# Other places in SBUF for the first row tiles of a kernel's last stage, and its last DRAM sums issued later

## The chip, the cores and the metric

The kernel runs on one core of a Trainium2 chip. The metric is the device time of one execution in microseconds. The core's engines work in parallel, each through its own instruction queue in order: TensorE (PE, matmuls, with its weight loads shown as PEld), VectorE (DVE), ScalarE (ACT), GpSimd (POOL) and SyncE (SP). In this kernel SP issues nearly all loads (DMA queue q1), and POOL issues stores and DRAM-to-DRAM transfers (DMA queue q0); 16 DMA engines carry them out.

## The reference, cut to what matters

```python
def _A_ref(x, dft_seq_re, dft_seq_im, dft_hid_re, dft_hid_im):
    a = jnp.einsum("bsd,ed->bse", x, dft_hid_re)
    b = jnp.einsum("bsd,ed->bse", x, dft_hid_im)
    return jnp.einsum("ts,bse->bte", dft_seq_re, a) - jnp.einsum("ts,bse->bte", dft_seq_im, b)

def _B_ref(x, W_gate, W_up, W_down):
    gate = jnp.einsum("bsd,df->bsf", x, W_gate)
    up = jnp.einsum("bsd,df->bsf", x, W_up)
    gate = gate * (gate > 0)
    h = gate * up
    return jnp.einsum("bsf,fd->bsd", h, W_down)

xn = _layernorm(x, axis=-1)
return x + _A_ref(xn, ...) + _B_ref(xn, ...)
```

Here x is 1 x 2048 x 640 (S=2048 tokens, D=640), and the gate has F=1728 columns. All is float32.

## The kernel before, in words

Every float32 product is made of three matmuls on split operands (`mm3`, lines 139 to 141): an operand is written as a high part (an ACT copy to fp32r, line 133) and a low part (a DVE subtraction, line 134), and high x high, high x low and low x high are added up in PSUM. One such split is a pair of instructions, first on ACT, then on DVE. On top of that the products are formed by a Strassen-like scheme with seven block products in place of eight (named B11, T1, T2, B21, B22, T3, T4), whose operands are sums and differences of blocks.

The work has three stages. **The first** computes the products with the sequence DFT, in four column chunks of 512 tokens; its results go to DRAM as `pq`. **The second**, the gate, runs 26 units (`gate_up(n)`, n = 0 to 25): 13 column blocks of F for the token half q=1, then 13 for q=0. Each unit loads weights into `z` (two pools, `z0` and `z1`, by turns), splits them into `gw0` or `gw1`, runs its products against the token sets, and POOL stores the result `ob` to `hd`. A remainder of F is done by `gate_up_rest`, at the beginning for q=1 and at the end for q=0. During the gate the weights of the last stage are prepared in tiles of pool `prep` and stored to `wparts` and `wquads` in DRAM. Near its end `lead_load` and `lead_split` (DVE, line 134, `gw<-st`) prepare unit 0 of the last stage from two tiles of pool `stage`.

**The last stage** (`project(q)`, first q=1, then q=0) multiplies `pq` and `hd` by the hidden DFT and by W_down. The contraction goes over seven units u: three of `hid`, two of `f`, one odd, and again `f` (in the code `UNITS`: hid (0,1), hid (2,3), hid (4), f (0,1), odd, f (2,3), f (4,5)). For each product name these seven units run in turn: for q=1 B11, T1, T2, B22 and so on. In TensorE's order unit 0 of B11 is the one from `lead_split`. A unit loads its row tile (`rw`, for the odd unit `ro`; lines 1249 to 1255) and its weights (`wt`, line 1281), DVE forms the difference of two rows (line 1304), and rows and weights are split into `cb` (a ring of four tiles, `ring2`) and `wt`. Finished sums are added to `y` on DVE (line 1217), and `y` is stored. Besides, `second_level` adds seven further products that read DRAM tiles `grown`, sums of `hd` blocks which POOL makes with accumulating DRAM-to-DRAM transfers (`grow`, lines 1144 and 1145).

The order in the last stage is written by hand for SP, POOL and PE (`drive_last`, a manual schedule): step by step, each unit's loads are issued six units ahead of its products and its splits are placed three units ahead. ACT and DVE are left to a scheduler, which decides at build time where the splits stand between the gate's last instructions. What an SP load waits for is set by two things: which of eight completion counters it takes over, and whose tile lay at its place in SBUF before.

SBUF is filled by pools that lie behind one another, left and right; a pool that opens later may lie over closed ones, and a tile then waits for the last reader of what it covers. By the sizes in the code (bytes per partition, from the end of pool `keep`) the left side during the gate is: gw0 0 to 17,408, stage to 25,600, r1 to 58,368, prep to 82,944, z0 to 92,672, wr to 97,792, tmp to 108,032, hob to 116,224, stage3 to 124,416, sets to 157,184, z1 to 166,912. When all of these are closed, the last stage puts over them: lead (six row tiles of 4,096, for B11's rows) 0 to 24,576, a gap, wts (seven weight tiles of 6,144) from 25,600 to 68,608, ring2 (four tiles of 8,192) to 101,376, raws (21 tiles of 4,096) to 187,392. Unit 0's row takes the highest place of `lead`, over both tiles of `stage`, and unit 1's the lowest, over gw0. The `odd` pool lies on the right, over the token set B22 in `xs_early`, which `gate_up_rest(0)` reads to its end.

Of the kernel before, what the change touches and what calls it, by code (L numbers as in the profile page):

```python
# [7 lines left out]
F32 = mybir.dt.float32  # L8
# [4 lines left out]
P = 128  # L13
S, D, F = 2048, 640, 1728
KD = D // P
CH = 512
# [16 lines left out]
AHEAD = 6  # L33
# [3 lines left out]
B11, B12, B21, B22, T1, T2, T3, T4, X4 = range(9)  # L37
# [28 lines left out]
def fnet_reglu_kernel(  # L66
# [15 lines left out]
    nc = tc.nc  # L82
# [18 lines left out]
    sets = [dram_p.tile([NSET, P, W2], F32, name=f"set{q}") for q in range(2)]  # L101
# [7 lines left out]
    grown = [dram_p.tile([4, P, n, CH], F32, name=f"grown{g}") for g, (_, _, n, _) in enumerate(GROUPS)]  # L109
# [44 lines left out]
    todo = []  # L154
# [681 lines left out]


    ph2 = ExitStack()
    for n, b, side in (("prep", 2, "left"), ("z0", 1, "left"), ("wr", 1, "left"), ("tmp", 1, "left"), ("hob", 2, "left"),
                       ("stage3", 2, "left"), ("sets", 1, "left"), ("z1", 1, "left"), ("gw1", 1, "right")):  # L840
        open_pools[n] = ph2.enter_context(tc.tile_pool(name=n, bufs=b, side=side, reuse_waits="tile"))
    pool = open_pools.__getitem__
    stage3 = lambda: pool("stage3").tile([P, W2], F32, name="st")
# [36 lines left out]
    tmp = lambda name, n=CH: pool("tmp").tile([P, n], F32, name=name)  # L880
# [12 lines left out]
    ending = []  # L893
# [203 lines left out]
    lead = {}  # L1097
# [36 lines left out]
    def quarter(q, g, half):  # L1134
        what, k, n, _ = GROUPS[g]
        if what == "hid":
            return pqd[2 * q][1][:, k + half * n : k + half * n + n]
        first = 2 * (k + half * n) + 1
        return hd[q][first : first + 2 * n - 1 : 2, :, :CH].rearrange("f p t -> p f t")

    def grow(g):

        t = [grown[g][i] for i in range(4)]
        put = lambda o, i: lambda: nc.gpsimd.dma_start(o, i)
        add = lambda o, i: lambda: nc.gpsimd.dma_start(o, i, accum_op=OP.add)
        return {"1": put(t[0], quarter(1, g, 0)), "1+": add(t[0], quarter(0, g, 0)), "3": put(t[2], quarter(0, g, 1)),
                "3+": add(t[2], quarter(0, g, 0)), "2": put(t[1], t[0]), "2+": add(t[1], quarter(0, g, 1)),
                "4": put(t[3], t[1]), "4+": add(t[3], quarter(1, g, 1))}

    behind_store = {n: [] for n in range(NU)}  # L1150
    for g, plan in enumerate((((10, "1 3"), (11, "1+"), (12, "3+"), (13, "2"), (14, "2+"), (15, "4"), (16, "4+")),
                              ((17, "1"), (18, "1+"), (19, "2"), (21, "3"), (22, "2+"), (23, "3+"), (24, "4"), (25, "4+")),
                              ((20, "1"), (24, "1+"), (25, "2"), (None, "3 2+ 3+ 4 4+")))):
        made = grow(g)
        for n, names in plan:
            (ending if n is None else behind_store[n]).extend(made[i] for i in names.split())
# [24 lines left out]
    ph0.close()  # L1181


    for n, b, side in (("lead", 6, "left"), ("gap", 1, "left"), ("wts", AHEAD + 1, "left"), ("ring2", 4, "left"), ("raws", 21, "left"),
                       ("odd", 4, "right"), ("y", 1, "right")):
        open_pools[n] = ctx.enter_context(tc.tile_pool(name=n, bufs=b, side=side, reuse_waits="tile"))

# [20 lines left out]
    def get_y(q, *which):  # L1208
        for e, c in which:
            own = f"{q}" if e in (0, 1, 4) and c == 0 else ""  # L1210
            y[q, e, c] = t = pool("y").tile([P, CH], F32, name=f"y{e}{c}{own}")
            nc.sync.dma_start(t, xt[e * P : (e + 1) * P, (2 * q + c) * CH : (2 * q + c + 1) * CH])
# [18 lines left out]
    def project(q):  # L1231
        c0, c1 = 2 * q, 2 * q + 1
        raws = {}
# [5 lines left out]
        def get(kind, u):  # L1239
            what, ks = UNITS[u]  # L1240
            if what == "odd":
                o = raws[kind, u] = pool("odd").tile([P, 1, CH], F32, name="ro")
            else:
                o = raws[kind, u] = pool("lead" if kind == "B11" else "raws").tile([P, 2, CH], F32, name="rw")[:, : len(ks)]
            col, row = int(kind in ("B12", "B22")), int(kind in ("B21", "B22"))
            if what == "odd":
                cs = slice(col * CH, (col + 1) * CH)
                if row:
                    nc.sync.dma_start(o[:REST, 0], hrest[q][:, cs])
                else:  # L1250
                    nc.sync.dma_start(o[:, 0], hd[q][NF - 1][:, cs])
            elif what == "hid":
                nc.sync.dma_start(o, pqd[(c0, c1)[col]][row][:, ks[0] : ks[-1] + 1])
            else:
                nc.sync.dma_start(o, hd[q][2 * ks[0] + row : 2 * ks[-1] + row + 1 : 2, :, col * CH : (col + 1) * CH].rearrange("f p t -> p f t"))

        def unit(name, u, first, last):
# [7 lines left out]
            def load():  # L1265
                kind = {"B11": "B11", "T1": "B12", "T3": "B21"}.get(name)
                if kind and (kind, u) not in raws and (name, q, u) != ("B11", 1, 0):
                    get(kind, u)
                ahead = {("T1", 2): 0, ("T1", 4): 1, ("T1", 6): 2, ("T2", 0): 3, ("T2", 2): 4, ("T2", 3): 5, ("T2", 4): 6}.get((name, u))
                if ahead is not None:  # L1270
                    get("B22", ahead)
                if (q, name, u) == (1, "B11", 1):
                    get("B11", 0)
                if q and name == "T2" and u in (1, 5):
                    get("B21", SINGLE[u // 5])
# [136 lines left out]
        for name, us in (("B11", every), ("T1", every), ("T2", every), ("B22", every[:4]), ("T3", every), ("B22", every[4:]), ("T4", every)):  # L1412
            for u in us:
# [5 lines left out]
                for kind, i, first, last in now:  # L1419
                    l, p, r, f = unit(kind, i, first, last)  # L1420
# [89 lines left out]
    alone = lambda f: (f, idle, idle, idle, idle)  # L1510
    quads = second_level()
    Y_AFTER = {(1, "T2", 5): ((4, 0),), (1, "T4", 5): ((0, 0), (1, 0))}
    for q in (1, 0):
        for steps, of in project(q):
            todo.extend(steps)
            if of in Y_AFTER:
                todo.append(alone((lambda which: lambda: get_y(0, *which))(Y_AFTER[of])))
            if of[:2] == (1, "T2") and ending:
                todo.append(alone(ending.pop(0)))
            if of in QUADS_AFTER:  # L1520
                todo.append(quads.pop(0))
    assert not quads and not ending
    with tc.manual_schedule(engines={mybir.EngineType.SP, mybir.EngineType.Pool, mybir.EngineType.PE}):
        drive_last()

# [38 lines left out]
```

## Time and profile before

| | |
|---|---|
| median of 3 runs | 1030.7 us (1030.24 to 1031.24) |
| profiled execution | 1031.5 us |
| its span (first to last instruction) | 1029.7 us |
| PE busy | 1020.5 us, 99% of the span |
| DVE busy | 824.8 us, 80% |
| ACT busy | 456.2 us, 44% |
| POOL busy | 117.8 us, 11% |
| mean granted TensorE clock | 0.996 |
| HBM read and written | 203.26 and 72.89 MB, 268 GB/s over the span |

The span is what the trace covers; the execution's own time is a little longer. "Busy" counts an engine's arithmetic, not the time in which it issues DMAs or waits on semaphores. A row of the timeline gives start, duration, engine, line and operation with output and input tiles, the number of instructions, and in brackets the idle time before it with what ended it. Matmuls are pipelined: one is shown 0.39 us long, and the next starts before it ends, so the rate is read from start to start. A row of waits gives engine, line and tile, what it waited for, the total in us, how often, and the longest. Issue rows of SP and POOL (SPq, POOLq) stand at the time of the issue, and a stretch merged into one row (x2) contains the waiting between its issues.

### The profile page before, as it was taken

How to read it: one execution, taken by the hardware profiler on the slowest of the kernel's cores; microseconds unless marked ns; L12 is line 12 of the kernel's file. 1: busy time of each engine (PE TensorE's matmuls, PEld its weight loads, DVE VectorE, ACT ScalarE, POOL GpSimd, SP SyncE). 2: the span in 40 equal slices, each digit the busy share in tenths (PEclk: the TensorE clock that was granted, in tenths of full speed). 3: DMA queues.
4: the chain of work that ended last, by engine and by line, in shares of the span. 5: the costliest groups of instructions: out<-in, count | busy, mean ns of one | idle time of the engine just before them, and what ended most of it. 6: DMA issues, size and time to landing. Idle time of an engine off the chain costs nothing.

```text
span 1029.7 us, 12759 instructions
## 1 busy us (share of the span) xinstructions
PE 1020.5 (99%) x4510; PEld 842.6 (82%) x4510; DVE 824.8 (80%) x1162; ACT 456.2 (44%) x588; POOL 117.8 (11%) x190
## 2 busy tenths in 40 slices
PE   9999999999999999999999999999999999999998
PEld 7888888888888888888888888888787888888887
DVE  7957977979879697778988878876388878598887
ACT  6664453333334443434446444443343555454552
POOL 2000010122110001321111111111100000000001
PEclk9999999999999999999999999999999999999999
DMA  9884744967859566775568889897797689999795
GB/s 333 326 271 161 261 158 126 358 224 233 333 200 364 198 206 201 246 247 187 221 223 282 283 304 337 288 316 206 223 395 260 208 265 311 325 323 324 219 282 167
DMA packets 113808, 267.57 MB, mean 260 GB/s; under 512 B 13104, under 2 KB 58096, under 8 KB 112112
## 3 DMA queue, kind: packets, MB, share of 16 engines
q1 hardware_dynamic: 92272, 178.77, 51.8%
q0 software_dynamic: 21040, 87.57, 24.6%
q8 instruction: 35, 0.57, 0.2%
q10 hardware_dynamic: 432, 0.43, 0.1%
q14 instruction: 29, 0.24, 0.1%
HBM read 203.26 MB, written 72.89 MB: 268 GB/s over the span
## 4 chain that ended last, share of the span: by engine, by line
PE 94%; DMA 3%; DVE 2%; ACT 1%; issue 0%; SPq 0%; ACTq 0%
PE ps L140 30%; PE ps L141 30%; PE ps L139 30%; PE ps L527 3%; DMA wt<-wparts 2%; PE ps L556 1%; DMA rw<-pq 1%; PE ps L1360 1%; DVE rw L1304 0%; DMA raw<-in_dft 0%; DVE cb L134 0%; DVE wt L134 0%; DVE y L1217 0%; DVE gw L134 0%; ACT cb L133 0%
## 5 line engine op out<-in xcount | busy, mean ns | idle before, releaser
L140 PE MATMUL ps<-cb,wt 128*128 128x512 f32 (+1 forms) x407 | 159.6, 392 | 2.2 <-DVE cb L134 2.1
L139 PE MATMUL ps<-cb,wt 128*128 128x512 f32 (+1 forms) x407 | 159.4, 392 | 1.8 <-ACT cb L133 1.8
L141 PE MATMUL ps<-cb,wt 128*128 128x512 f32 (+1 forms) x407 | 159.1, 391 | 0.0
L133 ACT ACTIVATE cb<-rw 128x1024 fp32r<-128x1024 f32 (+1 forms) x94 | 89.6, 961 | 87.0 <-PE ps L141 50.7
L134 DVE TENSOR_TENSOR cb<-rw,cb 128x1024 fp32r<-128x1024 f32 (+1 forms) x94 | 102.7, 1102 | 23.8 <-ACT cb L133 23.1
L133 ACT ACTIVATE cb<-raw 128x1024 fp32r<-128x1024 f32 x64 | 67.9, 1060 | 104.4 <-PE ps L141 98.0
L134 DVE TENSOR_TENSOR cb<-raw,cb 128x1024 fp32r<-128x1024 f32 x64 | 78.2, 1222 | 30.1 <-ACT cb L133 29.8
L139 PE MATMUL ps<-xs_early,gw 128*128 128x512 f32 x260 | 101.2, 389 | 0.0
L141 PE MATMUL ps<-xs_early,gw 128*128 128x512 f32 x260 | 101.2, 389 | 0.0
L140 PE MATMUL ps<-xs_early,gw 128*128 128x512 f32 x260 | 101.1, 389 | 0.0
L140 PEld LDWEIGHTS ps<-cb,wt 128*128 128x128 f32 x407 | 77.1, 189 | 19.9 <-DVE cb L134 4.1
L139 PEld LDWEIGHTS ps<-cb,wt 128*128 128x128 f32 x407 | 77.1, 189 | 18.7 <-ACT cb L133 2.6
L139 PE MATMUL ps<-cb,xs_late 128*128 128x512 f32 x232 | 90.2, 389 | 0.0
L140 PE MATMUL ps<-cb,xs_late 128*128 128x512 f32 x232 | 90.2, 389 | 0.0
L141 PE MATMUL ps<-cb,xs_late 128*128 128x512 f32 x232 | 90.2, 389 | 0.0
L141 PEld LDWEIGHTS ps<-cb,wt 128*128 128x128 f32 x407 | 77.1, 190 | 15.7
L139 PE MATMUL ps<-cb,xs_early 128*128 128x512 f32 x226 | 87.9, 389 | 0.0
L140 PE MATMUL ps<-cb,xs_early 128*128 128x512 f32 x226 | 87.9, 389 | 0.0
L141 PE MATMUL ps<-cb,xs_early 128*128 128x512 f32 x226 | 87.9, 389 | 0.0
L130 ACT ACTIVATE gw<-z 128x1024 fp32r<-128x1024 f32 (+1 forms) x52 | 56.4, 1110 | 37.1 <-PE ps L141 23.6
L130 ACT ACTIVATE u<-ps 128x512 f32<-128x512 f32 x52 | 31.1, 598 | 88.1 <-PE ps L141 74.2
L875 DVE TENSOR_TENSOR gw<-z,gw 128x1024 fp32r<-128x1024 f32 (+1 forms) x52 | 64.8, 1284 | 1.9 <-ACT gw L130 1.8
(209 smaller groups left out, 1990.7 us busy)
## 6 DMA issues: line engine op xcount, KB each, us to landing
raw<-in_dft SPq DMA_DIRECT2D x94, 512.0 KB, 5.8
wt<-wparts SPq DMA_DIRECT2D x74, 256.0 KB, 4.5
wparts<-pw POOLq DMA_DIRECT2D x12, 1408.0 KB, 7.2
z<-in_wgu SPq DMA_DIRECT2D x26, 640.0 KB, 6.1
rw<-hd SPq DMA_DIRECT2D x27, 512.0 KB, 6.6
hd<-ob POOLq DMA_DIRECT2D x26, 512.0 KB, 4.5
wt<-wparts SPq DMA_DIRECT2D x29, 384.0 KB, 5.3
rw<-pq SPq DMA_DIRECT2D x19, 512.0 KB, 5.9
```

Source lines behind the costliest of these rows:

```text
L130: return nc.scalar.activation(o, i, AF.Copy)
L133: nc.scalar.activation(hi, src, AF.Copy)
L134: return nc.vector.tensor_tensor(lo, src, hi.bitcast(F32), op=OP.subtract)
L139: nc.tensor.matmul(ps, wh, mh, start=first, stop=False, skip_group_check=more)
L140: nc.tensor.matmul(ps, wh, ml, start=False, stop=False, skip_group_check=more)
L141: nc.tensor.matmul(ps, wl, mh, start=False, stop=last, skip_group_check=more)
L527: nc.tensor.matmul(E[0, key], xn_part(n * SG + j, d)[v == 1], b[:, int(v == 2), j], start=False, stop=n % NH == NH - 1 and (j, v) == (SG - ...
L556: nc.tensor.matmul(E[c, key], xn_part(j, d)[v == 1], b[c][0][:, int(v == 2), j], start=j == 0 and v == 0, stop=False)
L875: tt(self.w[:, 1, cs], self.z[:, cs], self.w[:, 0, cs].bitcast(F32), op=OP.subtract)
L1360: nc.tensor.matmul(B[out], w[:, v, oo : oo + P], b, start=False, stop=last and v == 1, skip_group_check=more)
```

## The change

There are three edits, and a scheduler's answer to them.

First, the pools of the gate are opened in another order: z1 comes right behind z0. In the last stage a pool `low` of six row tiles takes the bottom, where `lead` was, and holds the rows of B12, the second column, which had been in `raws`; `lead` moves behind the weights, and `raws` has 15 tiles. By the sizes, z1 then lies at 92,672 to 102,400, wr to 107,520, tmp to 117,760, hob to 125,952, stage3 to 134,144, sets to 166,912, and over them low at 0 to 24,576, wts as before, lead at 68,608 to 93,184 (over prep, z0 and the first 512 bytes of z1), ring2 to 125,952 (z1, wr, tmp, hob), raws to 187,392.

Second, of the third group's `grown` tiles, the plain copy into tile 2 ("3" in the plan) is taken out of POOL's queue and issued by SP after the last unit of T2.

Third, the four transfers that follow it in POOL's queue ("3+", "2+", "4", "4+") are no longer spread over the units of T2; they stand behind that copy, and the first of them waits for it, since it adds to the same tile.

```diff
-    for n, b, side in (("prep", 2, "left"), ("z0", 1, "left"), ("wr", 1, "left"), ("tmp", 1, "left"), ("hob", 2, "left"),
-                       ("stage3", 2, "left"), ("sets", 1, "left"), ("z1", 1, "left"), ("gw1", 1, "right")):
+    for n, b, side in (("prep", 2, "left"), ("z0", 1, "left"), ("z1", 1, "left"), ("wr", 1, "left"), ("tmp", 1, "left"), ("hob", 2, "left"),
+                       ("stage3", 2, "left"), ("sets", 1, "left"), ("gw1", 1, "right")):
...
-                              ((20, "1"), (24, "1+"), (25, "2"), (None, "3 2+ 3+ 4 4+")))):
+                              ((20, "1"), (24, "1+"), (25, "2"), (None, "3+ 2+ 4 4+")))):
...
-    for n, b, side in (("lead", 6, "left"), ("gap", 1, "left"), ("wts", AHEAD + 1, "left"), ("ring2", 4, "left"), ("raws", 21, "left"),
+    for n, b, side in (("low", 6, "left"), ("gap", 1, "left"), ("wts", AHEAD + 1, "left"), ("lead", 6, "left"), ("ring2", 4, "left"), ("raws", 15, "left"),
                        ("odd", 4, "right"), ("y", 1, "right")):
...
-                o = raws[kind, u] = pool("lead" if kind == "B11" else "raws").tile([P, 2, CH], F32, name="rw")[:, : len(ks)]
+                o = raws[kind, u] = pool({"B11": "lead", "B12": "low"}.get(kind, "raws")).tile([P, 2, CH], F32, name="rw")[:, : len(ks)]
...
-            if of[:2] == (1, "T2") and ending:
-                todo.append(alone(ending.pop(0)))
+            if of == (1, "T2", 6):
+                todo.append(alone(lambda: nc.sync.dma_start(grown[2][2], quarter(0, 2, 1))))
+                todo.extend(alone(f) for f in ending)
```

PE's instructions stand in the same order as before. On ACT, at the end of the last gate unit (`ob` and `u` are its copies out of PSUM, `wt` the weights of units 2, 3 and odd of B11), the scheduler now places:

```order
 L133 ACTIVATE xs_early<-st 128x1024
 L130 ACTIVATE p_5635<-ps 128x512
+L133 ACTIVATE wt<-wt 128x384
+L133 ACTIVATE wt<-wt 128x2x384
+L133 ACTIVATE wt<-wt 128x384
 L130 ACTIVATE ob<-ps 128x512
 L130 ACTIVATE u_5636<-ps 128x512
```

Three weight splits have moved ahead of the gate's copy of `ob`; on DVE their low parts for units 2 and 3 have moved likewise, ahead of line 945 and of line 963.

On SP, at the end of the gate's loads, the rows are the same in both kernels; what they wait for is not. Before (5792 is the row of unit 1, 5794 that of unit 0, then units 2 and 3 and the odd unit; z_5477 is the last load of the gate):

```order
L855 DMA z_5477<-in_wgu 128x1280 [waits DMAHW7_49,DVE_49]
L1281 DMA wt_5790<-wparts_94 128x2x384 [waits DMAHW0_49,PE_49]
L1253 DMA rw_5792<-pq2_88 128x1024 [waits DMAHW1_49,DVE_49,PE_49]
L1253 DMA rw_5794<-pq2_88 128x1024 [waits DMAHW2_49,DVE_49]
L1281 DMA wt_5796<-wparts_94 128x384 [waits DMAHW5_49,DMAHW4_49,DMAHW6_49,DMAHW3_49,DMASW6_49]
L1253 DMA rw_5798<-pq2_88 128x512
L1281 DMA wt_5800<-wparts_94 128x2x384
L1255 DMA rw_5802<-hd1_91 128x2x512
L1281 DMA wt_5809<-wparts_94 128x384 [waits DMAHW7_49]
L1251 DMA ro_5811<-hd1_91 128x512 [waits DMAHW0_49,PE_49]
```

And now:

```order
L855 DMA z_5477<-in_wgu 128x1280 [waits DMAHW7_49,DVE_49]
L1281 DMA wt_5793<-wparts_94 128x2x384 [waits DMAHW0_49,PE_49]
L1253 DMA rw_5795<-pq2_88 128x1024 [waits DMAHW3_49,DMAHW2_49,DMAHW4_49,DMAHW1_49,DMAHW5_49,DMASW6_49,DMAHW6_49,DMASW3_49,DVE_49]
L1253 DMA rw_5797<-pq2_88 128x1024 [waits DMAHW7_49,DVE_49]
L1281 DMA wt_5799<-wparts_94 128x384
L1253 DMA rw_5801<-pq2_88 128x512
L1281 DMA wt_5803<-wparts_94 128x2x384
L1255 DMA rw_5805<-hd1_91 128x2x512
L1281 DMA wt_5812<-wparts_94 128x384
L1251 DMA ro_5814<-hd1_91 128x512 [waits DMAHW0_49,DVE_49,PE_49]
```

Unit 1's row no longer waits for PE but for stores out of `prep` (DMASW), and the DVE wait of unit 0's row is for the reader of z1 instead of `stage`; the odd unit's `ro` waits for PE as before.

On POOL, around the gate's last stores (grown_97 and grown_98 are the second and third group's sums, hd_90 the gate's result for q=0):

```order
 L1144 DMA grown_97<-grown_97 16x8192
 L1145 DMA grown_98<-hd_90 128x512
-L1144 DMA grown_98<-hd_90 128x512
 L889 DMA hd_90<-ob 128x1024
 L1145 DMA grown_97<-hd_91 256x1x512
```

The copy has gone from here and stands in SP's queue at line 1519, between the weights of the last unit of T2 and those of the first unit of B22.

More of the change, by code (lines that the diff above doesn't have):

```diff
@@ L1517, in fnet_reglu_kernel @@
                 todo.append(alone((lambda which: lambda: get_y(0, *which))(Y_AFTER[of])))
-            if of[:2] == (1, "T2") and ending:
-                todo.append(alone(ending.pop(0)))
+            if of == (1, "T2", 6):
+                todo.append(alone(lambda: nc.sync.dma_start(grown[2][2], quarter(0, 2, 1))))
+                todo.extend(alone(f) for f in ending)
             if of in QUADS_AFTER:
                 todo.append(quads.pop(0))
-    assert not quads and not ending
+    assert not quads
     with tc.manual_schedule(engines={mybir.EngineType.SP, mybir.EngineType.Pool, mybir.EngineType.PE}):
```

## The prediction

> **What bounds the kernel now.** I read the head of the page first, then TensorE's waits, then windows and timeline around each wait, and last the queue whose lateness caused them.
>
> ```profile
> span 1029.7 us, 12759 instructions
> ...
> PE 1020.5 (99%) x4510; PEld 842.6 (82%) x4510; DVE 824.8 (80%) x1162; ACT 456.2 (44%) x588; POOL 117.8 (11%) x190
> ```
>
> TensorE (PE) is the bound, and the change leaves its instructions as they are. All that can be won is time in which it waits or runs slow; the list of its waits says where that is (total, times, longest).
>
> ```profile
> PE ps L140 <- DVE cb L134: 2.1, 3, 1.5
> PE ps L139 <- ACT cb L133: 1.8, 1, 1.8
> ```
>
> Both belong to the last stage's first units. What they cost is more than these 3.9 us, as windows cut from the start of one matmul to the start of another show (length, PE busy, instructions, granted clock, DMA share, GB/s; the count takes in one or two matmuls at the edges):
>
> ```profile
> 733.56:738.10 4.54, 4.54 (x22) 1.00 1.03 362
> 738.10:746.56 8.46, 6.44 (x19) 0.80 1.08 336
> 763.14:764.54 1.40, 0.95 (x5) 1.00 1.05 401
> 775.90:783.18 7.28, 5.80 (x17) 0.77 1.08 358
> ```
>
> Matmuls start in turn at L139, L140, L141, so the starts in the timeline can be counted: 20 in the first window, 0.227 us each, which is full speed. The second has 18: 8.46 us where 4.09 were due, **4.4 lost**. The third has 3: 1.40 against 0.68, **0.7 lost**. The fourth has 16: 7.28 against 3.63, **3.6 lost**. Together **8.7 us**. More than half of it is the clock after the wait: mean 0.80 and 0.77 after waits of 1.8 and 1.5 us, and still 1.00 in the third window, where the wait was under half a microsecond.
>
> The cause is SyncE's queue (SP), which issues every load of this stage.
>
> ```profile
> 712.68 17.91 SPq L1253 DMA_DIRECT2D rw<-pq  x2
> 730.77 0.32 SPq L1281 DMA_DIRECT2D wt<-wparts  x1
> ```
> ```profile
> SPq L1253 <- DVE gw L134: 17.2, 1, 17.2
> ```
> ```profile
> 728.24 2.01 DVE gw L134 x2
> 730.27 8.29 DMA rw<-pq
> ...
> 749.55 8.57 DMA wt<-wparts
> 758.14 0.86 ACT wt L133
> ```
>
> The row of unit 0 has a place over the two `stage` tiles, which `lead_split` reads until 730.25; SP waits 17.2 us for that with the next load, and everything behind it is issued after 730.27. The chain of waits (the last fence) runs on through loads to 758.14 and then through VectorE (DVE) to the third stall. All three stalls are one lateness.
>
> **The change part by part.** *B11's rows over the gate's tiles.* Unit 1's row now waits for the last store out of `prep`, unit 0's for the last reading of `z1`:
>
> ```profile
> 699.81 0.55 POOL L1060 DMA_DIRECT2D wparts<-pw  x1 [6.86 <-DVE z L861]
> ```
> ```profile
> wparts<-pw POOLq DMA_DIRECT2D x1, 1408.0 KB, 5.0
> ```
> ```profile
> 703.77 2.48 DVE L875 TENSOR_TENSOR gw<-z,gw 128x1024 fp32r<-128x1024 f32 x2
> ```
>
> That is 699.8+5.0 = 704.8 and 703.77+2.48 = 706.25. Then SP can issue, some 0.4 us each, as far as the odd unit's `ro`, whose place lies over set B22, which TensorE reads until about 730. So seven loads stand at 705 to 709: rows of units 1, 0, 2, 3 (512+512+256+512 KB) and weights of 2, 3 and odd (192+384+192 KB), 2.6 MB. Unit 1's row was at 712.68 already; the other 2.1 MB stood behind 730. What follows `ro` is issued from 730.3 as before.
>
> Is that early enough for the rest? In the old run SP's queue (q1) moved almost nothing before 735, because POOL's (q0) had come first (727 to 735 us; packets, MB, share):
>
> ```profile
> q0 software_dynamic: 430, 1.29, 71.5%
> q1 hardware_dynamic: 12, 0.05, 1.8%
> ...
> hd<-ob POOLq DMA_DIRECT2D x1, 512.0 KB, 2.9
> ```
> ```profile
> 705.00:710.00 5.00, 5.00 (x24) 4.14 (x23) 2.82 (x3) 2.12 (x5) 0.18 (x1) 1.00 0.87 170
> 710.00:715.00 5.00, 5.00 (x24) 4.14 (x23) 3.34 (x5) 1.36 (x2) 0.58 (x2) 1.00 0.27 66
> 715.00:720.00 5.00, 5.00 (x24) 4.14 (x23) 0.47 (x1) 1.20 (x2) 1.92 (x3) 1.00 0.89 268
> 720.00:725.00 5.00, 5.00 (x24) 4.14 (x23) 2.08 (x3) 0.68 (x2) 0.00 (x0) 1.00 0.37 93
> 735.00:740.00 5.00, 3.48 (x16) 2.55 (x14) 0.56 (x1) 0.96 (x2) 1.76 (x2) 1.00 1.03 399
> 740.00:745.00 5.00, 4.50 (x12) 2.89 (x13) 2.87 (x3) 2.62 (x4) 0.52 (x1) 0.70 1.10 294
> 750.00:755.00 5.00, 5.00 (x24) 4.14 (x23) 3.97 (x5) 2.15 (x3) 0.80 (x1) 1.00 1.06 407
> 760.00:765.00 5.00, 4.55 (x20) 3.45 (x19) 5.00 (x7) 2.84 (x4) 0.00 (x0) 1.00 1.06 406
> ```
>
> (Busy time of PE, PEld, DVE, ACT, POOL, then clock, DMA share, GB/s.) From 735 on at the 0.40 MB/us of these rows, `ro` (0.26 MB) lands near 736; TensorE comes to the odd unit 27 matmuls, 6.1 us, after 738.3, at 744.4. Units 5 and 6 (1.8 MB) are in by 741 and are wanted at 746.5 and 750.6. Units 2 and 3, the old first stall, have been in since before 720. Their ring tiles now lie over `hob`, whose last store, issued at about 728, lands in 2.9 us, so near 731, and a split takes two microseconds of the seven that remain. **First stall gone: 4.4.**
>
> The weights that landed at 758.14 come 5.2 us sooner for the 2.1 MB that no longer stand ahead of them (752.9); by the plain sum of the bytes ahead (4.5 MB from 735) they come at 746.2. VectorE's chain took from 758.14 until TensorE went on at 778.27, 20.1 us, so the unit of the third stall is ready between 766.3 and 773.0. TensorE, 5.1 us ahead by the first two stalls, wants it at 771.2. I take the middle, 769.7, since the held-back sums leave that stretch as well. **Second and third stall gone: 4.3**; at the late bound about 1.8 us of waiting would stay (rival 2).
>
> *What is late next.* ACT's queue, which runs in order, now has three weight splits ahead of the gate's copy of `ob`. That copy must end before TensorE comes back to its bank, when the next block ends, at about 718.0 (the second row starts on it):
>
> ```profile
> 716.76 0.60 ACT L130 ACTIVATE ob<-ps 128x512 f32<-128x512 f32 x1 [5.40 <-PE ps L141]
> 718.12 0.60 ACT L130 ACTIVATE u<-ps 128x512 f32<-128x512 f32 x1 [0.76 <-PE ps L141]
> ```
>
> The third split needs the last of the seven loads. 2.6 MB take 6.5 us at 0.40. If they fill what a POOL sum leaves free from 707 to 711, they end at 716.4 (its share there would take 2.8 us of the time); if they start only behind it, near 717.3. A split (0.5) and the copy (0.6) follow: 717.5 to 718.4, a wait of 0 to 0.4 us. Should POOL's next wave (0.89 and 0.37 of two stretches, so until about 722) be served first, the load ends near 722 and the wait is 5 us (rival 1). I take 0.4: at 727 to 735 what stood first went first, and here SP's loads do.
>
> [...]
>
> *Places.* B12's six rows get places of their own and the others 15 for 21, the same total; a place comes back after 190 matmuls or more, 43 us, while loads run some six units ahead. Nothing; a wait of a few us in SP would still lie under that lead. *Start of the gate:* `stage3` now lies over `sa`, so ACT's first `st` waits for a store that so far only VectorE waited for:
>
> ```profile
> 405.63 1.28 DVE L994 TENSOR_TENSOR st<-ps,st 64x512 f32<-64x512 f32 x2 [1.84 <-DMA pq<-sa]
> ```
> ```profile
> 402.42 0.60 ACT L993 ACTIVATE st<-ps 64x512 f32<-64x512 f32 x1
> ...
> 410.70 0.60 ACT L130 ACTIVATE ob<-ps 128x512 f32<-128x512 f32 x1 [2.53 <-PE ps L141]
> ```
>
> ACT's row moves from 402.4 to 405.6, the copy of `p` behind it by some tenths. TensorE needs `p` when the block before the `ob` copy is done, at 410.7: nothing, under 3 us of cover; without the cover, up to 3.2 us.
>
> *Sums.* One copy leaves POOL for SP: 0.4 us of issue where SP waits for TensorE anyway. Four transfers leave 737 to 757 for 780 to 805 (rival 3).
>
> **Sum.** 1029.7 - 8.7 + 0.4 = 1021.4 us of span. The profiled execution took 1031.5 for its span of 1029.7; the median of the runs, 1030.7, is 1.0 above that span, so the forecast is **1022.4 us**.
>
> **The rivals.** *1, a new wait at the gate's end.* POOL's wave is served before the early weights: 5 us of waiting and some 2.2 of slow clock, as after the old stalls, in place of 0.4: 1029.2, half of it 1025.8. For it: q0 did starve q1 after 730. Against it: there q0 was first. [...] *2, only the first stall goes.* The change does half of what it says: `ro` still holds SP until 730, weights and VectorE stay late: 1030.7-4.4+0.4 = 1026.7, or 1024 to 1026 if one stall shrinks. For it: VectorE at 5.00 of 5.00. Against it: 3.1 MB less to move before 757. *3, slower.* The held-back transfers run at 780 to 805 and SP's loads get nothing beside them. From 736 to 758 they took:
>
> ```profile
> grown<-hd POOLq DMA_DIRECT2D x3, 256.0 KB, 7.2
> grown<-grown POOLq DMA_DIRECT2D x1, 256.0 KB, 6.3
> ```
>
> 3x7.2+6.3 = 28 us one after another. Weights run six units of T2 ahead (12 matmuls, 2.7 us each), 16 us; from that point TensorE waits, 12 us: 1034.4. Against it: beside such sums, at 740 to 745, all queues still moved 294 GB/s.
>
> **How the numbers follow.** Forecast 0.62 (1021.2 to 1023.8), rival 1 0.17 (1023.8 to 1029), rival 2 0.15 (1024 to 1027), rival 3 0.05, something else 0.01. To hold 8 in 10 the range goes from 1021.2 to 1026.8. A measurement of this kernel tells about 0.2%, 2 us, from no change: faster 0.92, same 0.03, slower 0.05.
>
> **What would show it.** Right: SP issues seven loads between 704 and 710, no wait of TensorE above 0.5 us after 730, granted clock 1.00 to the end, POOL's four transfers after 775. Wrong: ACT waits for `wt` at 712 to 722 and TensorE is idle near 718 (rival 1); VectorE is full from 750 and TensorE idle near 770 (rival 2); TensorE is idle after 785 (rival 3).

## The result

The changed kernel takes **1024.6 us** (median of four executions, 1024.2 to 1025.2) against 1030.5 for the kernel before on the same chip: a ratio of 0.9942, with a 95% interval of 0.9925 to 0.9959. It is faster by 5.9 us. The forecast was 1022.4, so 2.2 us are missing.

The page of the changed kernel answers to the first lines shown of before. The profiled execution took 1024.17 us for this span:

```profile
span 1022.4 us, 12767 instructions
...
PE 1016.7 (99%) x4510; PEld 841.6 (82%) x4510; DVE 824.4 (81%) x1162; ACT 455.5 (45%) x588; POOL 117.3 (11%) x189
```

TensorE's waits, the whole list (total, times, longest). The two waits for `cb` are gone; the first row is the start of the kernel, and the second is new:

```profile
PE ps L121 <- DVE warm L117: 1.1, 1, 1.1
PE ps L139 <- ACT ob L130: 1.0, 1, 1.0
```

The windows that held the three stalls (length, PE busy, ..., granted clock, DMA share, GB/s) are full, at full clock:

```profile
738.10:746.56 8.46, 8.46 (x39) 6.99 (x38) 4.79 (x6) 4.66 (x6) 0.00 (x0) 1.00 1.04 402
763.14:764.54 1.40, 1.40 (x8) 1.17 (x7) 1.40 (x3) 0.28 (x1) 0.00 (x0) 1.00 1.07 388
775.90:783.18 7.28, 7.28 (x34) 6.03 (x33) 4.91 (x8) 1.69 (x2) 0.00 (x0) 1.00 1.02 333
```

SP's queue in the timeline (start, us, what) shows why: seven loads at 705 to 709, where before SP stood still from 712.7 to 730.3 with one issued. The last row is `ro`, which still waits until the 730s:

```profile
705.09 1.69 SPq L1253 DMA_DIRECT2D rw<-pq  x2
706.83 0.45 SPq L1281 DMA_DIRECT2D wt<-wparts  x1
707.33 0.54 SPq L1253 DMA_DIRECT2D rw<-pq  x1
707.92 0.56 SPq L1281 DMA_DIRECT2D wt<-wparts  x1
708.52 0.54 SPq L1255 DMA_DIRECT2D rw<-hd  x1
709.11 0.47 SPq L1281 DMA_DIRECT2D wt<-wparts  x1
731.80 0.33 SPq L1251 DMA_DIRECT2D ro<-hd  x1
```

The new wait lies where the gate ends. ACT's timeline there: three weight splits, each of them waiting for its load, and right behind the third the copy of `ob`.

```profile
714.68 0.53 ACT L133 ACTIVATE wt<-wt 128x384 fp32r<-128x384 f32 x1 [3.14 <-DMA wt<-wparts]
716.33 0.85 ACT L133 ACTIVATE wt<-wt 128x768 fp32r<-128x768 f32 x1 [1.12 <-DMA wt<-wparts]
718.17 0.52 ACT L133 ACTIVATE wt<-wt 128x384 fp32r<-128x384 f32 x1 [0.99 <-DMA wt<-wparts]
718.60 0.58 ACT L130 ACTIVATE ob<-ps 128x512 f32<-128x512 f32 x1
```

TensorE's own timeline beside it:

```profile
717.87 0.39 PE L141 MATMUL ps<-sets_b,gw 128*128 128x512 f32 x1
719.23 0.50 PE L139 MATMUL ps<-xs_early,gw 128*128 128x512 f32 x1 [0.97 <-ACT ob L130]
719.57 0.39 PE L140 MATMUL ps<-xs_early,gw 128*128 128x512 f32 x1
```

From start to start 1.36 and 0.34 us, where 0.227 each were due: 1.25 us lost. POOL's four held-back transfers run where they were put, with no wait of TensorE near them:

```profile
786.88 1.74 POOL L1145 DMA_DIRECT2D grown<-hd  x2 [52.83 <-DMA grown<-hd]
794.65 0.52 POOL L1144 DMA_DIRECT2D grown<-grown  x1 [6.03 <-DMA grown<-hd]
798.68 0.81 POOL L1145 DMA_DIRECT2D grown<-hd  x1 [3.52 <-DMA grown<-grown]
```

So the trace shows the mechanism that was predicted, with one term too small. Three questions were left for the chip: which half of the change does the work; what makes the last early load late; and what a wait of TensorE really costs.

### The profile page after: what moved, and what is told of

Its sections match the earlier page's. It is cut to its first block, busy times and chain, and to the rows that moved or that the text cites. A ratio compares the mean times of both kernels' runs of the same rounds, so it can differ in the third digit from the quotient of the medians.

```text
span 1022.4 us, 12767 instructions
## 1 busy us (share of the span) xinstructions
PE 1016.7 (99%) x4510; PEld 841.6 (82%) x4510; DVE 824.4 (81%) x1162; ACT 455.5 (45%) x588; POOL 117.3 (11%) x189
```

## The experiments

Times are medians; the kernel before was timed again beside each group of runs and had 1030.3, 1030.5, 1030.2 and 1031.7 us.

### The changed kernel again, and its two halves

> The changed kernel once more, as the measure for the three beside it. Expected: 1024.6 us (1024.2 to 1025.2), a ratio of 0.994 to the kernel before; TensorE waits 1.0 us for the copy of `ob` near 718 and nowhere else after the start.

Measured: 1024.27 us (1024.15 to 1025.14), 0.994 of the kernel before (0.9926 to 0.9953), as expected; the wait for the copy of `ob` is 1.3 us in this profile. It is the measure for what follows.

The places without the sums:

```
-((20, "1"), (24, "1+"), (25, "2"), (None, "3+ 2+ 4 4+"))
+((20, "1"), (24, "1+"), (25, "2"), (None, "3 2+ 3+ 4 4+"))
...
-if of == (1, "T2", 6):
-    todo.append(alone(lambda: nc.sync.dma_start(grown[2][2], quarter(0, 2, 1))))
-    todo.extend(alone(f) for f in ending)
+if of[:2] == (1, "T2") and ending:
+    todo.append(alone(ending.pop(0)))
```

> The changed kernel without the edit of the sums: the copy of group 2's third piece stands on POOL behind the gate as before, and the four transfers run beside T1 and T2's first loads, at 737 to 757. Theory (the early loads alone take the 2.1 MB out of the way, and the held-back sums are a help of about a microsecond at most): all three stalls gone, 1024.6 to 1026.5 us. Rival (it is the sums that make room for T1's weights): first stall gone, second and third stay, 1024.6+4.3 = 1028.9 us.

Measured: 1024.37 us, ratio 0.994 (0.9928 to 0.9953), the same as the whole change. No wait for `cb` is left near the three stalls; the one in TensorE's list (the last row here) ends at 908.41, far behind them:

```profile
PE ps L139 <- ACT ob L130: 1.0, 1, 1.0
PE ps L140 <- DVE cb L134: 0.3, 1, 0.3
```

What is left near the stalls is too short for that list: matmuls start at 751.94, 752.42 and 752.76, 0.37 us lost. The places alone remove all three stalls. The rival, that the sums make room for T1's weights, is out.

The sums without the places (the pools of the gate and of the last stage as in the kernel before):

```
-("low", 6, "left"), ("gap", 1, "left"), ("wts", AHEAD + 1, "left"), ("lead", 6, "left"), ("ring2", 4, "left"), ("raws", 15, "left")
+("lead", 6, "left"), ("gap", 1, "left"), ("wts", AHEAD + 1, "left"), ("ring2", 4, "left"), ("raws", 21, "left")
...
-pool({"B11": "lead", "B12": "low"}.get(kind, "raws"))
+pool("lead" if kind == "B11" else "raws")
```

> The kernel before with the edit of the sums alone: places as before, so SP is held until 730. Theory: the first stall stays with its 4.4 us, and with 1 MB of transfers fewer ahead of them T1's weights come some 2.5 us sooner, which takes 0.7 and most of 3.6 us: 1026.5 to 1028 us, with a wait of 1.8 us near 738 and less than 1 us near 776. Rival (the sums do nothing for the stalls): 1030.5 us with all three waits; or, if the lateness behind 730 were itself due to the sums, 1024 to 1026 us.

Measured: 1027.20 us (1026.89 to 1027.59), ratio 0.9967 (0.9954 to 0.9979), in the middle of the theory's range. TensorE's waits:

```profile
PE ps L140 <- DVE cb L134: 1.6, 3, 0.8
PE ps L139 <- ACT cb L133: 1.5, 1, 1.5
```

The first stall stays, and the last one ends at 775.45 instead of 778.27. So the sums are worth 3 us in the old layout and nothing once the loads are early: both edits remove the same lateness, and the places remove all of it.

Which of the new places counts? One exchange of names puts B11's rows back over the `stage` tiles and leaves B12 with six places of its own:

```
-pool({"B11": "lead", "B12": "low"}.get(kind, "raws"))
+pool({"B11": "low", "B12": "lead"}.get(kind, "raws"))
```

> The changed kernel with two names exchanged: the first rows (B11) take the six places over the `stage` tiles, as in the kernel before, and the second column's rows (B12) the six places over `prep` and `z`. Places of their own for both, the order of the queues and the held-back sums stay. Theory (SP's wait for the `stage` tiles is the whole cause): SP is held until 730 again, and the time is that of the sums alone, 1027.2 us (1026.9 to 1027.6). Rival (places of B12's own have a share in the gain): between 1024.3 and 1026.5 us with SP held all the same.

Measured: 1027.56 us (1026.76 to 1028.36), ratio 0.9973 (0.9963 to 0.9983), the time of the sums alone. SP is held as in the kernel before:

```profile
712.60 17.92 SPq L1253 DMA_DIRECT2D rw<-pq  x2
730.70 0.32 SPq L1281 DMA_DIRECT2D wt<-wparts  x1
```

Which tiles the first row lies over is the whole gain; a place of its own for each row of the second column is worth nothing that shows here.

### The new wait: ACT's queue

```
-        copy(u3, b1)
+        late["gate"] = copy(u3, b1).ins
...
-        split(w[:, :, 0], w[:, :, 1], w[:, :, 1].bitcast(F32))
+        with tc.issue_after(late["gate"]):
+            split(w[:, :, 0], w[:, :, 1], w[:, :, 1].bitcast(F32))
```

> The changed kernel, but the four weight splits of the last stage's first units stand behind the gate's last three copies on ACT instead of ahead of them. Theory (the wait at 718 is ACT's queue, held by the last early load): that wait goes, with its 1.25 us, and nothing is late in its place, because the splits are wanted at 738 and ACT is idle from 724: 1023.3 us, 1.2 under the changed kernel. Rival (the block that TensorE needs there is ready no earlier, or the splits come late for the first units at 734 to 746): 1024.6 us or more, with a wait near 718 or near 738.

Measured: 1023.03 us (1022.56 to 1023.51; the changed kernel beside it 1024.15 to 1025.14), ratio 0.9925 (0.9913 to 0.9938). ACT's copies stand alone now, the splits follow in the gap:

```profile
717.09 0.60 ACT L130 ACTIVATE ob<-ps 128x512 f32<-128x512 f32 x1 [5.17 <-PE ps L141]
...
722.39 2.39 ACT L133 ACTIVATE wt<-wt 128x768 fp32r<-128x768 f32 x4
```

The wait at 718 is gone, with 1.24 us, and no other wait of TensorE in the list of this profile lies behind it. The theory holds, and this kernel is faster than both.

With the wait at 718 out of the way, the sums could be judged once more (this kernel with the sums as before the change; the edit is that of the places without the sums):

> The kernel with the splits behind the copies (1023.0 us), but with the sums as before the change: the copy on POOL behind the gate, the four transfers at 737 to 757. Theory (once the early loads are in, the held-back sums only take away a wait of some 0.4 us near 752): 1023.4 us. Rival (they do nothing that shows): 1023.0 us. Third (they carry more than the places alone showed, since the wait at 718 hid it): 1024 us or more.

Measured: 1022.99 us (1022.71 to 1023.64), ratio 0.9928 (0.9916 to 0.9941). The held-back sums do nothing that shows.

### What made the last load late

First attempt: take POOL's copy and sum away from 714.6.

```
-..., (23, "3+"), (24, "4"), (25, "4+")), ((20, "1"), (24, "1+"), (25, "2"), (None, "3+ 2+ 4 4+"))
+..., (23, "3+"), (None, "4 4+")), ((20, "1"), (25, "1+ 2"), (None, "3+ 2+ 4 4+"))
```

> The changed kernel, but the copy and the sum that POOL issued right behind the store at 714.6 are moved: the sum of group 2 behind the next store, at 729, and the copy and its sum of group 1, with the second copy of group 2, to the transfers that are held back until 780. Only the store of 0.5 MB is left at 714.6. The weight splits stay ahead of the copy of `ob`. Theory (the last early load came 1 us late since it shared the DMA engines with POOL's wave, 0.96 MB of POOL's against 0.79 of SP's from 714.5 to 718.2): the last load lands before 717, no wait at 718, 1023.1 us, the same as with the splits behind the copies. Rival (the loads were late from their start on, because POOL's sum from 704 held the engines until 709): the last load lands after 717.5 and 0.6 us or more of the wait stay, 1023.9 to 1024.6 us.

Measured: 1032.38 us (1030.38 to 1034.05), ratio 1.0017 (1.0008 to 1.0026), slower than the kernel before. The edit did not do what it says. In the built program the copy and its sum stand further forward on POOL, not behind (POOL's timeline):

```profile
700.49 0.52 POOL L1144 DMA_DIRECT2D grown<-grown  x1 [7.32 <-DMA grown<-hd]
701.27 0.56 POOL L1060 DMA_DIRECT2D wparts<-pw  x1 [0.26 <-issue]
...
712.82 1.09 POOL L1145 DMA_DIRECT2D grown<-hd  x1 [7.42 <-issue]
```

The copy stands ahead of the store out of `prep`, so SP's first load, which waits for that store, is issued at 708.98 instead of 705.09. The queues from 704.64 to 711.04 (packets, MB, share of 16 engines) have POOL's q0 alone, no SP load (q1) at all:

```profile
q0 software_dynamic: 487, 2.11, 102.6%
```

And ACT's third split, with the copy of `ob` behind it, comes 5.5 us later than in the changed kernel:

```profile
723.69 0.52 ACT L133 ACTIVATE wt<-wt 128x384 fp32r<-128x384 f32 x1 [4.61 <-DMA wt<-wparts]
724.12 0.58 ACT L130 ACTIVATE ob<-ps 128x512 f32<-128x512 f32 x1
```

TensorE's row among the waits:

```profile
PE ps L139 <- ACT ob L130: 6.4, 1, 6.4
```

By accident this is what the prediction's first rival describes, in full size, though here SP itself starts 3.9 us later. As a test of the wave at 714.6 it says nothing.

Second attempt, with both behind the gate's last store:

```
-..., (23, "3+"), (24, "4"), (25, "4+")), ((20, "1"), (24, "1+"), (25, "2"), (None, "3+ 2+ 4 4+"))
+..., (23, "3+"), (25, "4 4+")), ((20, "1"), (25, "1+ 2"), (None, "3+ 2+ 4 4+"))
```

> The changed kernel, but POOL's copy of group 1 and sum of group 2 stand behind the gate's last store, at 729, in place of the last but one, at 714.6; nothing else moves, and on POOL nothing new stands ahead of 714.6. Behind that store SP has 0.79 MB left to load, 2.0 us at 0.40 MB/us, and shares the engines with the 0.5 MB of the store alone. Theory (the wave made the last load late): it lands between 716.5 and 717.7, so the wait near 718 shrinks from 1.0 us to between 0 and 0.6: 1023.1 to 1024.0 us. Rival (what POOL issued before 711 is what counts): the load lands near 718 as before, 1024.3 us. A third way: the heavier wave at 729 makes `ro` late, with a new wait of TensorE near 744.

Measured: 1025.77 us (1025.20 to 1027.31), ratio 0.9953 (0.9939 to 0.9966). In this profile everything at the gate's end stands 1.0 us later than in that of the changed kernel (SP's first early load is at 706.11), since TensorE lost that microsecond in three short stalls at 319 to 332. The third split:

```profile
719.21 0.52 ACT L133 ACTIVATE wt<-wt 128x384 fp32r<-128x384 f32 x1 [0.86 <-DMA wt<-wparts]
```

That is 718.2 in the times of the other profile: the last load is as late as with the wave. The theory falls, and the third way came on top, a wait for `cb` near 749 (0.8 of the second row of TensorE's waits here, the rest is one of the stalls near 320; 1.4 us are lost near 749, counted by starts):

```profile
PE ps L139 <- ACT ob L130: 1.0, 1, 1.0
PE ps L140 <- DVE cb L134: 1.0, 2, 0.8
```

What is left is what POOL issued before 711. In the changed kernel, the queues from 706.2 to 711.0:

```profile
q0 software_dynamic: 224, 0.45, 61.4%
q1 hardware_dynamic: 167, 0.62, 37.9%
```

POOL's sum from 704 takes three fifths of the engines' time for 0.45 MB, and SP's loads move 0.62 MB in 4.8 us. So the last run moves this sum alone:

```
-(22, "2+"), (23, "3+"), (24, "4"), (25, "4+")
+(22, "2+"), (24, "3+ 4"), (25, "4+")
```

> The changed kernel with one transfer moved: the 0.5 MB sum that POOL issued behind the store at 703.6 stands behind the next store, at 714.6, in front of the wave that is there. SP's queue and ACT's order stay. Theory, formed on the windows of the changed kernel (from 706.2 to 711.0 that sum held 55 to 67% of the DMA engines' time for 0.46 MB, and SP's loads moved 0.62 MB where 0.39 MB/us would have made 1.9): without it the 2.6 MB are in by 713 to 714, before the store at 714.6; the third split is done by 715, no wait near 718, 1023.0 us as with the splits behind the copies. The wave at 714.6 is then heavier by some 5 us, where the engines were idle from 722 to 729. Rival (the store at 714.6 or the landing of the loads themselves sets it): the third split still starts after 717.5 and 0.6 us or more of the wait stay, 1023.8 us or more. Third: the heavier wave runs into the loads behind 730, with a new wait of TensorE near 744 to 749 as in the run with the wave moved, 1024.4 us or more.

Measured: 1022.91 us (1022.57 to 1023.67), ratio 0.992 (0.9907 to 0.9934), level with the splits behind the copies. The same window of the queues (706.2 to 711.0) has SP alone, with 1.31 MB:

```profile
q1 hardware_dynamic: 477, 1.31, 86.7%
```

ACT's third split is done before the copy of `ob` is due, and the copy waits for TensorE again instead of the other way round:

```profile
715.89 0.53 ACT L133 ACTIVATE wt<-wt 128x384 fp32r<-128x384 f32 x1 [0.87 <-DMA wt<-wparts]
716.85 0.60 ACT L130 ACTIVATE ob<-ps 128x512 f32<-128x512 f32 x1 [0.43 <-PE ps L141]
```

The theory holds in cause and time. One of its numbers does not: the load was to be in by 714 and landed at 715.9, since 1.31 MB in 4.8 us is 0.27 MB/us and not 0.39.

### What a wait costs

> The kernel before, profiled once more, without any edit. The profile that the prediction worked from had a span of 1029.7 us; the other executions of the same kernel had 1028.2 to 1030.6, with a median of 1028.5, while the time of every execution stands 1.8 us over its own span. Theory: the three stalls themselves differ from execution to execution, because the clock does not halve after each of these waits: in a profile near 1028.5 the same three waits are there, together 7 to 8 us lost in place of 8.7. Rival: the stalls lose 8.7 us again, and what differs lies elsewhere, at the start of the kernel.

Measured: span 1030.0 us, the rival. TensorE's waits for `cb` in this execution:

```profile
PE ps L140 <- DVE cb L134: 3.6, 4, 1.5
PE ps L139 <- ACT cb L133: 1.3, 1, 1.3
```

The windows around the three stalls (length, PE busy, ..., granted clock, DMA share, GB/s):

```profile
738.06:746.56 8.50, 6.17 (x24) 3.98 (x23) 4.05 (x6) 4.61 (x7) 0.90 (x2) 1.00 1.08 336
761.96:764.35 2.39, 1.22 (x4) 0.48 (x3) 2.39 (x4) 1.74 (x3) 0.00 (x0) 1.00 1.05 404
775.93:783.23 7.30, 5.81 (x18) 4.06 (x16) 7.30 (x8) 3.42 (x4) 0.00 (x0) 0.77 1.07 360
```

The clock stays at 1.00 behind the first wait this time. Counted by matmul starts the three lose 3.3, 1.7 and 3.7 us: 8.7 again, where the other profile had 4.4, 0.7 and 3.6. The first stall was a microsecond shorter, the second longer by that microsecond, and TensorE goes on after the third at 778.3 in both. The stalls are not three separate costs: what was lost before 778 is set by the chain that ends there.

Five copies more on ACT ahead of the copy of `ob`, on the kernel with the splits behind the copies, and the same with eight:

```
+        if n == NU - 1:
+            for _ in range(5):
+                copy(u3, b4)
         copy(ob[:, c1], b4)
```

> The kernel with the splits behind the copies (1023.0 us, no wait at 718), and in it five copies that nobody reads on ACT ahead of the copy of `ob` in the gate's last unit, 0.5 us each, 2.5 us against a slack of 0.8: TensorE waits 1.7 us near 718, at a place where nothing else is late. What does the wait cost beyond its length? Theory (after a wait of 1.5 us or more TensorE runs about 3.3 us at half clock, as in the profile of the kernel before): 1.7 us more, 1026.4 us, granted clock 0.5 in the 3 us behind the wait. [...] Third (it depends on where the wait falls): single executions in two groups, 1.7 us apart.

> The same with eight such copies: 4.0 us against the slack of 0.8, a wait of 3.2 us. Theory: 1.7 us of slow clock behind it, 1027.9 us. [...] Third: two groups as before, with more of the executions in the slower one.

Measured with five: 1027.29 us (1025.34 to 1027.75), ratio 0.9963 (0.9951 to 0.9976). The wait came out longer than meant:

```profile
PE ps L139 <- ACT ob L130: 2.4, 1, 2.4
```

From start to start (718.25, 721.03, 721.36) it costs 2.66 us, which makes 1025.7 with no slow clock and 1027.4 with 1.7 us of it. The five executions are at 1025.34 with a mean granted clock of 1.000, 1026.61 with 0.999, and 1027.29, 1027.49 and 1027.75 with 0.998. One stretch of half clock as long as that shown below for the kernel before (3.41 us) takes 0.0017 from the mean. The one with the profile is that at 1026.61, and the 3.5 us behind its wait run at full clock:

```profile
721.03:724.50 3.47, 3.47 (x15) 2.89 (x16) 0.69 (x1) 0.44 (x1) 0.00 (x0) 1.00 0.14 24
```

With eight: 1029.27 us (1028.74 to 1030.49), ratio 0.999 (0.9981 to 0.9999). The wait is 4.3 us, and the 4.0 us behind it hold 10 matmuls where full speed has 18 (4.55 us from start to start and 1.7 of slow clock make 1029.3):

```profile
722.50:726.49 3.99, 3.99 (x10) 3.12 (x11) 0.00 (x0) 0.44 (x1) 0.00 (x0) 0.57 0.00 0
```

So the third answer fits in its two groups: behind the 2.4 us wait the profiled execution had no half clock, and three others, by their times and mean clocks, had it; of those there is no profile. The execution at 1026.61 is 0.9 us over 1025.7: 0.7 of it are two short stalls of TensorE near 895 and 909, and 0.2 were there before the wait (718.25 against 718.02).

In the first profile of the kernel before, behind the 1.8 us wait, the clock stands at 0.50 from 741.98 to 745.39 and at 1.00 behind that:

```profile
741.98:745.39 3.41, 3.38 (x8) 2.15 (x7) 1.63 (x2) 1.58 (x2) 0.52 (x1) 0.50 1.10 261
745.39:748.81 3.42, 3.42 (x16) 2.81 (x15) 2.07 (x3) 2.31 (x3) 0.00 (x0) 1.00 1.05 406
```

The length of a wait alone does not tell whether half clock follows. Waits of 1.5 us were followed by it in both profiles of the kernel before (0.77 over the third stall's window) and not with the sums alone (1.00 from 738.08 to 746.56). A wait of 1.9 us (rows exchanged, the matmuls behind it start 0.23 us apart) and that of 2.4 us were not followed by it; those of 4.3 and 6.4 us were (0.57 from 722.50 to 726.49 with eight copies, 0.52 from 724.75 to 729.88 in the run of 1032.4 us). What decides is not shown, the place of the wait that the third answer names included.

## Why the prediction was right, and where it was off

**The cause was right.** SP's wait for the `stage` tiles held the loads, and which tiles the first row lies over decides it: with B11 over `stage` again, the gain shrinks to that of the sums, 1027.56. The places alone give 1024.37. The time itself, 1024.6, lies outside what the prediction gave its forecast (1021.2 to 1023.8) and among the ranges of rivals 1 and 2; 1.25 of the missing 2.2 us come from a median compared with one span, 0.85 from the new wait.

**First stall 4.4, second and third 4.3: right as a sum, wrong as separate terms.** All 8.7 us are gone from the profile. The unit of the third stall, forecast for 769.7, is ready at 768.77, when its split on DVE ends, and TensorE takes it at 772.63:

```profile
767.55 1.22 DVE L134 TENSOR_TENSOR cb<-rw,cb 128x1024 fp32r<-128x1024 f32 x1
```

But they were one chain's end and not three prices: a first stall that was a microsecond shorter bought nothing in the second profile of the kernel before. Rival 2 (first stall alone, 1026.7) was priced on that error: by this reading, with the chain to 778 as late as before, TensorE would only have waited longer there. No run takes the first stall away alone.

**"More than half of it is the clock after the wait" was read from one execution.** In another the clock behind the first wait stayed at 1.00, and the loss was the same 8.7 us, since TensorE had to wait for the next unit anyway. The executions of the kernel before that were timed beside the runs say the same: of 52, the 22 with a mean granted clock of 1.000 have a median of 1030.27 us, the 19 with 0.998 (about one stretch of half clock) have 1030.24, and the five with 0.996 (two) have 1031.68. In these executions half clock in front of a later wait on the same chain cost nothing that shows (1030.24 against 1030.27); by this reading only behind the last stall can it be a cost of its own. That it came behind the waits of 1.8 and 1.5 us holds for those two waits of that execution: 1.9 us with the rows exchanged and 2.4 us with five copies passed at full clock.

**"What is late next", taken at 0.4, measured 1.25: the term that was too small.** The place, the mechanism and the deadline were right (ACT's third split in front of the copy of `ob`, 718.0). The failed step is "if they fill what a POOL sum leaves free from 707 to 711, they end at 716.4", and in it the 0.40 MB/us, not the share of the sum. The 2.8 us reckoned for the sum were about right: it held 61.4% of 4.8 us, which is 2.9, and without it the third split began 2.3 us sooner, at 715.89. By 711 the step leaves SP 0.48 MB (1.2 us at 0.40), and 0.62 were moved. The rest, in the changed kernel from 711.0 to 717.4, took too long:

```profile
q1 hardware_dynamic: 1091, 2.00, 82.4%
```

That is 0.31 MB/us, and 2.0 MB at 0.40 would have ended at 716.0. With nothing of POOL's beside them the loads made no more: 1.31 MB from 706.2 to 711.0, which is 0.27, and 1.11 MB from 711.0 to 714.2, 0.35, as in the changed kernel. The 0.40 came from rows behind 735; why these loads are slower stays open. The last split began at 718.17. The prediction looked at the wave at 714.6 for the danger; moving its copy and sum away changed nothing at 718, while the 0.5 MB store stayed there. Without the sum from 704 only 0.15 MB of the loads are left at 714.2, just ahead of that store, and the wait is gone.

The choice of 0.4, "at 727 to 735 what stood first went first, and here SP's loads do", rested on 430 packets against 12. SP had issued nothing for the first 3 of those 8 us. In the changed kernel 224 packets of POOL's moved beside 167 of SP's in the same 4.8 us, from 706.2 to 711.0; why the two stretches differ is not shown.

**The span came out at 1022.4 instead of 1021.4:** 0.85 of the difference is this wait, and about 0.15 was there before it: the matmul ahead of the wait starts at 717.87, where the profile of before has 717.70.

**"+1.0, median over profiled span" was wrong in kind.** Every execution's time stands 1.8 us over its own span, before and after (1031.5 over 1029.7; 1024.17 over 1022.4). The 1.0 mixed that with the fact that the profiled execution of the kernel before was 0.8 us slower than its median. Taking it over assumed that the changed kernel's profile would be as slow against its median; it was the fastest of its four, 0.45 under the median. Added up: 1022.4 + 0.85 + 0.15 + 0.8 + 0.45 = 1024.65, measured 1024.62.

**Places, start of the gate, held-back sums at nothing: right**, as was rival 3's small chance: at 786 to 799 POOL's four transfers run and TensorE waits for nothing. The sums were put at nothing for the right reason only in part. They do shorten the old chain, by 3 us when they stand alone; the prediction used them only as a reason for taking the middle of a range.

**What it asked to be shown:** seven loads between 704 and 710, no wait after 730, clock 1.00 to the end and the four transfers after 775 are all in the profile. So is the sign it named for rival 1, "ACT waits for `wt` at 712 to 722 and TensorE is idle near 718", at a quarter of the 5 us.

## What to carry to other kernels

When loads are issued earlier, ask which in-order queue they land in front of: a split hoisted with its load can hold a copy that TensorE is due to need, and pinning it behind that copy (or moving the one transfer that the load shares the engines with) was worth 1.2 to 1.4 us of the 7.3 to be had. Stalls that end on one chain are priced once, by the moment at which the chain ends, and not one by one. When a forecast is made against a profiled execution, compare span with span and time with time, and see first where that execution lies among the others.

## What the runs showed that was not expected

- POOL's sum into DRAM beside the early loads cost them more than its bytes: 0.45 MB of it took 61.4% of the DMA engines' time for 4.8 us (0.15 MB/us for the engine time it held), while SP's loads beside it made 0.62 MB in 37.9% (0.34 MB/us).
- Half clock did not go by the length of the wait: waits of 1.9 and 2.4 us passed without it, and one of 1.5 us in the kernel before did not (0.77 from 775.90 to 783.18).
- Moving a transfer to a later place in the program text moved it earlier on POOL (700.5 instead of behind 714.6), ahead of a store that SP waits for; SP's loads, 3.9 us later for it and behind POOL's traffic, made a kernel that is slower than both, at 1032.4 us.
